# High-position tables of the S4 kernel in two tiles, one per half of a column quarter

## The chip, the cores and the metric

The kernel runs on one core of one Trainium2 chip. Its time is the device time of one execution in microseconds (us): the median of three runs is 391.03 us, the lowest 388.97 and the highest 391.36. The engines are named as in the profile: PE is TensorE, DVE is VectorE, ACT is ScalarE, POOL is GpSimd and SP is the engine that issues most of the DMAs. "SPq" and "POOLq" are the DMA queues filled from SP and POOL.

## The reference: linear attention beside an S4 convolution

The output is two independent results side by side, each 2048 x 448. The first is a hedgehog linear attention with 16 heads of 28. The second is an S4 layer: a long convolution whose kernel is a sum of 256 damped rotations for each of 448 channels.

```python
def _A_ref(x, wqkv, w_phi, wo):
    q, k, v = ...                       # x @ wqkv, split into 16 heads of 28
    pq = jnp.einsum("bhsd,hdf->bhsf", q, w_phi)
    pk = jnp.einsum("bhsd,hdf->bhsf", k, w_phi)
    phi_q = jnp.concatenate([_softmax(pq, axis=-1), _softmax(-pq, axis=-1)], axis=-1)
    phi_k = jnp.concatenate([_softmax(pk, axis=-1), _softmax(-pk, axis=-1)], axis=-1)
    kv = jnp.einsum("bhsf,bhsd->bhfd", phi_k, v)
    z  = jnp.einsum("bhsf->bhf", phi_k)
    num = jnp.einsum("bhqf,bhfd->bhqd", phi_q, kv)
    den = jnp.einsum("bhqf,bhf->bhq", phi_q, z)[..., None] + 1e-6
    return (num / den) ... @ wo

def _B_ref(u, A_re, A_im, B_re, B_im, C_re, C_im, log_dt, Dskip):
    dt = jnp.exp(log_dt)[:, None]
    logdA = dt * (A_re + 1j * A_im)
    dB = dt * (B_re + 1j * B_im)
    l = jnp.arange(L).astype(A_re.dtype)                        # bfloat16
    P = jnp.exp(logdA[:, :, None] * l[None, None, :])
    K = jnp.einsum("dn,dnl,dn->dl", Cc, P, dB).real
    y = irfft(rfft(K padded to 2L) * rfft(u padded to 2L))[:L]  # causal convolution
    return y + u * Dskip
```

The positions `l` are rounded to bfloat16 before they are used. Above 256 many of the 2048 positions therefore fall on the same value, and only 641 different positions are left. The kernel computes K at these 641 positions and lets the DFT matrices sum the repeats.

## The kernel before

**Positions.** Each of the 641 positions is the sum of a high position and a low offset, so that exp(dt A l) is a product of a high table and a low table, and the sum over the 256 states becomes a matmul: the high table is its weights, the low table is what is streamed. There are 16 high positions (16, 48, ..., 496; `HI`, L41) and 49 low offsets (`LO`, L36 to L39): plus and minus the 16 magnitudes 1 to 16 of `LO_ABS` (L33), 0, and 16 more offsets that are shifted by 512, 1024 or 1536.

**Columns.** The 448 channels are worked in four quarters (`qt`) and each quarter in two halves (`c`) of 56 channels. 128 of the 256 states lie on the partitions; the two sets of 128 are kept side by side, so a half has 112 columns and a quarter 224.

**One quarter of K** goes through these steps:

- `rotations` (L382): TensorE multiplies the angles by odd numbers (L373) and ScalarE takes sines and cosines of multiples (L389, L391) into the tile `T`, for all magnitudes. It is issued one quarter ahead.
- `dampings` (L397): TensorE again (L373), and ScalarE's exponentials go into the tile `W` (L404 for one magnitude, L407 for two or four). Two copies with a changed sign (L410, L411) follow for each half.
- `damp` (L413): VectorE multiplies exponentials by sines and cosines in place (L419), then makes the shifted offsets by multiplying with the power PW512 (L425 to L428). That completes the low tables of a half.
- `hi_tables` (L430): VectorE copies the first high position from `CB` (L433) and doubles the table four times with complex products (`cmul`, L286 to L293) by the powers PW32, PW64, PW128 and PW256. The result is `U[qt % 2][c]`: there are four tiles of 16 positions, two for the even and two for the odd quarters (L365).
- `build_k` (L444): TensorE, 224 matmuls a half (L453), with 16 columns of weights each and 49 streamed columns. Four column strips of the array hold four channels. The sums of a half lie in two PSUM tiles (`KB`, L698, set to zero once at L700), and ScalarE copies each to `Ts` (L457).
- `scatter_k` (L559): 24 DMAs bring `Ts` into the tile `Kt`, in which the positions lie on the partitions (`K_ROWS`, L42; one more row for a single position, L570).

**After K.** `kernel_spectrum` (L580) multiplies `Kt` by DFT tiles: each group of columns takes 16 tiles, seven matmuls from each (L593), and ScalarE copies the sums out (L596). The tiles are loaded by SP (`load_f`, L578) into the slots `RING` and `LATE`; four of the `LATE` slots lie directly behind the five powers in memory (L671). `conv_group` (L598) multiplies the spectra on VectorE (L610 and the sums behind it), TensorE transforms back (L634, L636), ScalarE copies out (L641) and SP stores (L645).

**The other work.** `signal_spectrum` (L217) loads blocks of u (issued by POOL), forms sums and differences on VectorE (L224, L225), and multiplies by DFT tables (L236); ScalarE or VectorE copies out (L239). Two buffers of u alternate, so a load waits for the L225 of two blocks before. `key_side` (L459) and `query_side` (L496) are the attention: in the latter, L501 and the exponentials L504 are followed by a small matmul (L510), VectorE's reciprocals (L517 on), and in each of four row blocks by matmuls (L529), VectorE's scaling (L532), a turn on TensorE (L539), a copy (L541) and the matmul with `wo` (L545).

**Order.** `rank(p)` (L679) gives the work inside it a priority. A planner goes through all instructions with these priorities and its own estimates of durations, and fixes the order of each engine before the program runs. On the chip every engine takes its instructions in that order. The ranks are: the key side 9000, the first fold of weights 8000, the high tables of quarter 0 10000, the four query sides 10500, quarter `qt` of K 11000 + 5000 `qt`, the first two kernel spectra 70000, the tail from 80000.

```python
for qt in range(4):
    with rank(11000 + 5000 * qt):
        ...
        dampings(qt)
        for c in range(2):
            damp(qt, c)
        for c in range(2):
            build_k(qt, c, Ts)
        if qt < 3:
            rotations(qt + 1)
            for c in range(2):
                hi_tables(qt + 1, c)
```

## Time and profile before

| measure | value |
|---|---|
| median of three runs | 391.03 us |
| the profiled execution: time | 391.03 us |
| the profiled execution: span, first to last instruction | 389.2 us |
| mean granted clock of TensorE | 0.855 of full speed |
| POOL busy | 34.1 us (9%) |
| matmuls of `build_k`, L453 | 1,792, 49.3 us busy |
| largest groups of VectorE: L419; L425; L610 | 37.4; 35.6; 24.4 us |
| complex products of powers and tables, L286 and L287 | 20.1 and 19.8 us |
| data moved | 31.60 MB, mean 81 GB/s |

All times inside the program are read from one profiled execution, and a time of the form "at 138.5" counts from the start of its span. The page of the profile gives for each engine its busy time and its share of the span, then the span in 40 slices with a digit of busy tenths for each engine (a slice is 9.73 us here). Groups of instructions are given by the line of the code, the engine and the operation; behind the bar stand the busy time of the group in us and the mean of one instruction in ns, then the idle time of the engine just before these instructions and the instruction that ended most of it. A row in order of time gives the start, the duration, and in brackets how long the engine had stood idle and for what. The chain of waits is followed back from the last instruction, at each step to whatever released it.

The granted clock is what the throttle allowed TensorE. It varies within the span; the mean over the span is in the table.

### The profile page before, as it was taken

The page shows a single profiled execution, that of the slowest core. Times are in us where ns is not written, and L with a number is a line of the kernel's source. Part 1 is how long each engine was busy: PE and PEld are TensorE (multiplying, and loading weights), DVE is VectorE, ACT ScalarE, POOL GpSimd, SP SyncE. Part 2 cuts the span into 40 slices and gives each one's busy share as a digit, 9 for nine tenths or more (in the row PEclk, how much of TensorE's full clock was granted, in tenths as well). Part 3 has the DMA queues.
Part 4 walks back from the last instruction along what each step waited for, and adds up shares of the span by engine and source line. Part 5 has one row for each costly group of instructions (what it writes and reads, how often), then busy time and mean ns, then how long its engine had stood idle before and what let it go on. Part 6 is the DMA issues. An engine that isn't in the chain of part 4 may idle for free.

```text
span 389.2 us, 9018 instructions
## 1 busy us (share of the span) xinstructions
PE 282.2 (73%) x3780; PEld 204.2 (52%) x3780; DVE 310.9 (80%) x548; ACT 219.1 (56%) x381; POOL 34.1 (9%) x59
## 2 busy tenths in 40 slices
PE   0294478988863859996787799677970596956994
PEld 0261353455452335674554576445860485945994
DVE  0598988999961279996459988998996979999872
ACT  1289972055554764799985846942949323212431
POOL 7100220000033000000000000001000000054000
PEclk9999569999995687999659699885986888796999
DMA  7990212200012001213000100120922218397005
GB/s 184 284 254 28 63 28 72 94 24 2 0 30 64 28 25 45 70 56 96 26 24 25 25 28 26 24 79 24 278 97 56 52 52 290 104 205 180 14 3 189
DMA packets 31105, 31.60 MB, mean 81 GB/s; under 512 B 11560, under 2 KB 28680, under 8 KB 30680
## 3 DMA queue, kind: packets, MB, share of 16 engines
q1 hardware_dynamic: 24216, 22.65, 20.1%
q0 software_dynamic: 4064, 7.23, 7.2%
q10 hardware_dynamic: 2784, 1.15, 1.3%
q8 instruction: 29, 0.48, 0.5%
q14 instruction: 12, 0.10, 0.1%
HBM read 23.07 MB, written 7.34 MB: 78 GB/s over the span
## 4 chain that ended last, share of the span: by engine, by line
PE 37%; DVE 20%; ACT 17%; DMA 11%; issue 7%; SPq 4%; POOL 3%; DVEq 0%; POOLq 0%; ACTq 0%
PE kb L453 10%; PE mmt L593 6%; DMA sbuf<-in_B_u_dram 5%; PE mmt L545 4%; PE mmt L236 3%; PE yo L634 3%; SPq L567 3%; ACT sbuf L504 3%; DVE sbuf L475 3%; DMA sbuf<-SUd 3%; PE mmt L501 3%; PE arg L373 2%; PE mmt L539 2%; DMA sbuf<-const 2%; DVE sbuf L239 2%
## 5 line engine op out<-in xcount | busy, mean ns | idle before, releaser
L453 PE MATMUL kb<-sbuf 128*16 128x49 bf16 x1792 | 49.3, 274 | 3.7 <-issue 2.9
L593 PE MATMUL mmt<-sbuf 128*128 128x112 bf16 (+1 forms) x336 | 34.4, 272 | 22.2 <-ACT sbuf L596 9.7
L419 DVE TENSOR_TENSOR sbuf<-sbuf 128x112 bf16<-128x112 bf16 (+1 forms) x64 | 37.4, 619 | 13.2 <-ACT sbuf L404 12.8
L453 PEld LDWEIGHTS <-sbuf 128*16 128x16 bf16 x1792 | 41.5, 118 | 9.4 <-issue 7.8
L236 PE MATMUL mmt<-sbuf 128*128 128x448 bf16 x128 | 34.0, 390 | 14.2 <-DVE sbuf L224 6.5
L593 PEld LDWEIGHTS <-sbuf 128*128 128x128 bf16 x336 | 28.6, 118 | 28.5 <-issue 11.2
L425 DVE TENSOR_TENSOR sbuf<-sbuf 128x896 bf16<-128x896 bf16 (+1 forms) x48 | 35.6, 775 | 0.2
L596 ACT CAST sbuf<-mmt 128x448 bf16<-128x448 f32 x32 | 16.2, 549 | 27.1 <-PE mmt L593 27.1
L634 PE MATMUL yo<-sbuf 128*128 128x112 bf16 (+1 forms) x384 | 28.8, 228 | 2.9 <-DMA sbuf<-const 1.8
L471 ACT ACTIVATE sbuf<-pkv 128x448 bf16<-128x448 f32 x32 | 15.8, 552 | 26.5 <-PE acc L485 19.1
L532 DVE TENSOR_TENSOR sbuf<-mmt,sbuf 128x448 bf16<-128x448 f32 x32 | 19.4, 622 | 11.0 <-PE mmt L529 10.7
L634 PEld LDWEIGHTS <-sbuf 128*128 128x128 bf16 x384 | 26.1, 98 | 3.5 <-DMA sbuf<-const 2.0
L610 DVE TENSOR_TENSOR sbuf<-sbuf 128x1792 bf16<-128x1792 bf16 (+1 forms) x18 | 24.4, 1400 | 3.5 <-ACT sbuf L596 3.3
L407 ACT ACTIVATE sbuf<-arg 128x896 bf16<-128x896 f32 (+1 forms) x32 | 25.8, 874 | 1.4 <-PE kb L453 1.4
L236 PEld LDWEIGHTS <-sbuf 128*128 128x128 bf16 x128 | 13.1, 106 | 19.9 <-issue 11.5
L641 ACT CAST sbuf<-yo 128x224 bf16<-128x224 f32 (+1 forms) x24 | 9.0, 410 | 25.2 <-PE yo L636 25.2
L373 PE MATMUL arg<-sbuf 128*128 128x224 bf16 x128 | 22.0, 320 | 1.3 <-ACT sbuf L404 0.7
L504 ACT ACTIVATE sbuf<-mmt 112x512 bf16<-112x512 f32 x32 | 17.2, 601 | 9.8 <-PE mmt L501 9.6
L545 PE MATMUL mmt<-sbuf 112*128 112x448 bf16 x64 | 19.6, 436 | 3.6 <-ACT sbuf L541 3.5
L501 PE MATMUL mmt<-sbuf 112*112 112x512 bf16 x64 | 19.4, 426 | 1.9 <-ACT sbuf L504 1.9
L286 DVE TENSOR_TENSOR sbuf<-sbuf 128x1792 bf16<-128x1792 bf16 (+3 forms) x33 | 20.1, 609 | 0.7
L287 DVE TENSOR_TENSOR sbuf<-sbuf 128x1792 bf16<-128x1792 bf16 (+3 forms) x33 | 19.8, 603 | 0.0
(117 smaller groups left out, 590.5 us busy)
## 6 DMA issues: line engine op xcount, KB each, us to landing
sbuf<-const SPq DMA_DIRECT2D x32, 224.0 KB
SUd<-sbuf SPq DMA_DIRECT2D x16, 224.0 KB
sbuf<-const SPq DMA_DIRECT2D x2, 1024.0 KB
sbuf<-in_A_x_dram SPq DMA_DIRECT2D x4, 448.0 KB
out_dram<-sbuf SPq DMA_DIRECT2D x16, 112.0 KB
sbuf<-SUd POOLq DMA_DIRECT2D x1, 1792.0 KB, 12.6
sbuf<-in_B_u_dram SPq DMA_DIRECT2D x4, 448.0 KB
sbuf<-SUd POOLq DMA_DIRECT2D x2, 896.0 KB, 9.2
```

The costliest lines, as they stand in the source:

```text
L236: mm(p[:, 0:D_MODEL].rearrange("p (q g x) -> p q g x", q=4, g=4), lhsT=G1[:, cp, jt, 128 * mt:128 * mt + 128], rhs=by_quarter(ab[:, cp ^ s ...
L373: mm(p[:, e // 2, (e % 2) * QC:(e % 2 + 1) * QC], lhsT=PID[:, 4 * grp + e, :], rhs=src[:, part, cols], start=(part == 0), stop=(part == 1))
L407: act(dst.rearrange("p c (a b) x -> p a b c x", b=2), src.rearrange("p a b (c x) -> p a b c x", c=2), ACT.Exp, scale=float(sgn * f))
L419: TT(out=W[:, c, cs_, r, :], in0=W[:, c, cs_ if sgn < 0 else 0, r, :], in1=T[:, cs_, j0:j0 + n, xs], op=ALU.mult)
L425: TT(out=(t2[:, :, 0:n, :], dst)[1 - i], in0=src, in1=PW[512][:, i, cols].unsqueeze(1).unsqueeze(1).to_broadcast([128, 2, n, COLS]), op=AL ...
L453: mm(p[32 * g:32 * g + N_HI, qq * N_LO:(qq + 1) * N_LO], lhsT=U[qt % 2][c][:, :, ri, xc], rhs=W[:, c, ri, :, xc], start=(i == 0), stop=(i ...
L501: mm(p[:, :], lhsT=WpQ[:, dj, 112 * c:112 * c + 112], rhs=xT[:, dj, 512 * sc:512 * sc + 512], start=(dj == 0), stop=(dj == 3))
L504: act(EQ[:, s, c, :], p[:, :], ACT.Exp, scale=1.0 - 2.0 * s)
L545: mm(pf[:, :], lhsT=oT_[:, c, :], rhs=wo[:, c, :], start=(c == 0), stop=(c == 3))
L593: mm(p[:, k2, :].rearrange("p (q g x) -> p q g x", q=nq, g=4), lhsT=f_tiles[i][1][:, fi, :], rhs=natural(Kt[:, kt, :], gi), start=(n == 0) ...
L610: TT(out=t[:, :, :], in0=su, in1=sk, op=ALU.mult)
L634: mm(p[:, k2, :], lhsT=GI[r][:, cp, mt, 128 * jt:128 * jt + 128], rhs=S[:, r, cp, mt, :], start=(cp == 0 and mt == 0), stop=False)
```

## The change

The high tables get 32 positions: the 16 of before, eight from 544 in steps of 64, and eight from 1088 in steps of 128. The last 16 are made from the first 16 by three more complex products in `hi_tables`, with the powers PW528, PW544 and PW512; the first two of these powers are new and are made once, from PW512 with PW16 and PW32. The new powers lie in memory where four `LATE` slots of the DFT tiles come later.

`U` is no longer four tiles of 16 positions, chosen by the quarter's parity and half, but two tiles of 32, one for each half. Each is rewritten for the next quarter when the matmuls of its own half have ended. The memory is the same 28,672 bytes on a partition.

The low offsets are 0 and plus and minus 24 magnitudes: the old 16 and 20, 24, 28, 32, 40, 48, 56, 64. All come from exponentials and sines of ScalarE, so `EVALS` has more rows (the fifth number is the step between target rows) and `T` holds 24 magnitudes. `damp` has no shifts by PW512 any more, and its products take 24, 15 and 9 magnitudes at a time. There are still 49 offsets.

`build_k` uses 32 columns of weights in place of 16, all 32 rows of a strip are written, and its PSUM tile is allocated anew for each half of a half; the two tiles set to zero are gone. `Kt` is filled by 28 DMAs in place of 24, since one of its row blocks comes from two runs of offsets. The DFT tiles are renumbered; each still takes seven matmuls.

```diff
-N_HI = 16
+N_HI = 32
...
-LO_ABS = [1, 3, 5, 7, 9, 11, 13, 15, 2, 6, 10, 14, 4, 12, 8, 16]
+LO_ABS = [1, 3, 5, 7, 9, 11, 13, 15, 2, 6, 10, 14, 4, 12, 8, 16, 24, 32, 40, 48, 56, 64, 20, 28]
...
-HI = [16 + 32 * a for a in range(N_HI)]
-K_ROWS = [(0, 0, 8, 0, 16), (1, 0, 8, 16, 32), (2, 8, 16, 16, 32), (3, 0, 16, 33, 41), (4, 0, 16, 41, 49)]
+HI = ([16 + 32 * a for a in range(16)] + [544 + 64 * a for a in range(8)] + [1088 + 128 * a for a in range(8)])
+K_ROWS = [(0, 0, 8, [(0, 16)]), (1, 0, 8, [(16, 32)]), (2, 8, 16, [(16, 32)]), (3, 16, 24, [(24, 36), (45, 49)]),
+          (4, 24, 32, [(28, 44)])]
...
-    PW = {k: sb(f"PW{k}", [128, 2, NCOL], BF16, oPW + 3584 * i) for i, k in enumerate((32, 64, 128, 256, 512))}
+    PW = {k: sb(f"PW{k}", [128, 2, NCOL], BF16, oPW + 3584 * i) for i, k in enumerate((32, 64, 128, 256, 512, 528, 544))}
...
     cmul(CB[:, :, :], CR[:, :, :], pw_all(16), tp[:, :, :])
+    cmul(PW[528][:, :, :], PW[512][:, :, :], pw_all(16), tp[:, :, :])
+    cmul(PW[544][:, :, :], PW[512][:, :, :], pw_all(32), tp[:, :, :])
...
-    U = [[sb(f"U{b}{c}", [128, N_HI, 2, COLS], BF16, oU + 14336 * b + 7168 * c) for c in range(2)] for b in range(2)]
+    U = [sb(f"U{c}", [128, N_HI, 2, COLS], BF16, oU + 14336 * c) for c in range(2)]
...
-    EVALS = [[(0, 4, 1, 0), (0, 4, 2, 8), (0, 2, 4, 12), (0, 1, 8, 14), (0, 1, 16, 15)], [(0, 4, 1, 4)]]
+    EVALS = [[(0, 4, 1, 0, 1), (0, 4, 2, 8, 1), (0, 2, 4, 12, 1), (2, 2, 4, 22, 1), (0, 4, 8, 14, 2), (0, 2, 16, 15, 4),
+              (0, 1, 32, 17, 1), (0, 1, 64, 21, 1)],
+             [(0, 4, 1, 4, 1)]]
...
     def dampings(qt):
...
         for c in range(2):
-            act(W[:, c, 1, 1:30:2, :], W[:, c, 0, 1:30:2, :], ACT.Copy, scale=-1.0)
-            act(W[:, c, 1, 32, :], W[:, c, 0, 32, :], ACT.Copy, scale=-1.0)
-
-    def damp(qt, c):
+            act(W[:, c, 1, 1:2 * N_ABS:2, :], W[:, c, 0, 1:2 * N_ABS:2, :], ACT.Copy, scale=-1.0)
+
+    def damp(c):
         xs = slice(c * COLS, (c + 1) * COLS)
-        n1 = N_ABS - 1
-        for j0, n, sgn in ((0, n1, -1), (n1, 1, -1), (0, n1, 1), (n1, 1, 1)):
-            r = w_rows(j0, n, sgn)
+        for j0, n, sgn in ((0, N_ABS, -1), (0, 15, 1), (15, N_ABS - 15, 1)):
+            r = w_rows(j0, n, 1, sgn)
             for cs_ in (1, 0):
                 TT(out=W[:, c, cs_, r, :], in0=W[:, c, cs_ if sgn < 0 else 0, r, :], in1=T[:, cs_, j0:j0 + n, xs], op=ALU.mult)
-        cols = slice((2 * qt + c) * COLS, (2 * qt + c + 1) * COLS)
-        for d0, s0, n in ((33, 24, 8), (41, 37, 4), (45, 41, 4)):
-            src, dst = W[:, c, :, s0:s0 + n, :], W[:, c, :, d0:d0 + n, :]
-            t2 = sb("t2", [128, 2, 8, COLS], BF16, oT2)
-            for i in (1, 0):
-                TT(out=(t2[:, :, 0:n, :], dst)[1 - i], in0=src, in1=PW[512][:, i, cols].unsqueeze(1).unsqueeze(1).to_broadcast(
-                    [128, 2, n, COLS]), op=ALU.mult)
-            TT(out=dst[:, 0], in0=dst[:, 0], in1=t2[:, 1, 0:n, :], op=ALU.add)
-            TT(out=dst[:, 1], in0=dst[:, 1], in1=t2[:, 0, 0:n, :], op=ALU.subtract)
...
     def hi_tables(qt, c):
         cols = slice((2 * qt + c) * COLS, (2 * qt + c + 1) * COLS)
-        U_ = U[qt % 2][c]
+        U_ = U[c]
...
         step(256, U_[:, 0:8], U_[:, 8:16], 8)
+        step(528, U_[:, 0:16:2], U_[:, 16:24], 8)
+        step(544, U_[:, 16:24:2], U_[:, 24:28], 4)
+        step(512, U_[:, 24:28], U_[:, 28:32], 4)
 
     def build_k(qt, c, Ts):
         for hq in range(2):
-            p = KB[hq]
+            p = ps_t.tile([128, 512], F32, name="kb", tag="kb", bufs=2)
...
-                        mm(p[32 * g:32 * g + N_HI, qq * N_LO:(qq + 1) * N_LO],
-                           lhsT=U[qt % 2][c][:, :, ri, xc],
+                        mm(p[32 * g:32 * g + 32, qq * N_LO:(qq + 1) * N_LO], lhsT=U[c][:, :, ri, xc],
                            rhs=W[:, c, ri, :, xc], start=(i == 0), stop=(i == 3), tile_position=(0, 32 * g))
...
     def scatter_k(gi, Ts, engs):
...
-        for kt, h0, h1, l0, l1 in K_ROWS:
-            for g in range(4):
-                engs[i % len(engs)].dma_start(out=dst(0, 128, kt, g), in_=Ts[32 * g + h0:32 * g + h1, l0:l1, :])
-                i += 1
+        for kt, h0, h1, runs in K_ROWS:
+            r = 0
+            for l0, l1 in runs:
+                n = (h1 - h0) * (l1 - l0)
+                for g in range(4):
+                    engs[i % len(engs)].dma_start(out=dst(r, n, kt, g), in_=Ts[32 * g + h0:32 * g + h1, l0:l1, :])
+                    i += 1
+                r += n
...
-                terms = [(0, 0), (1, 1), (2, 2), (3, 3), (4, 5)] if b == 0 else [(5, 3), (6, 4)]
+                terms = [(i, i) for i in range(5)] if b == 0 else [(5, 4), (6, 5)]
...
-    KB = [ps_t.tile([128, 512], F32, name="kb", tag="kb", bufs=2) for _ in range(2)]
-    for p in KB:
-        nc.vector.memset(p[:, :], 0.0)
```

## The prediction, made before the result was known

> **What bounds the kernel now.** I read the page's busy totals and slices first, then the groups by form, then VectorE's and ScalarE's instructions in order of time, and last the chain of waits.
>
> ```profile
> PE 282.2 (73%) x3780; PEld 204.2 (52%) x3780; DVE 310.9 (80%) x548; ACT 219.1 (56%) x381; POOL 34.1 (9%) x59
> DVE  0598988999961279996459988998996979999872
> ACT  1289972055554764799985846942949323212431
> PE 37%; DVE 20%; ACT 17%; DMA 11%; issue 7%; SPq 4%; POOL 3%; DVEq 0%; POOLq 0%; ACTq 0%
> ```
>
> No engine alone is the bound, but VectorE is full in most slices; its holes are at slices 12 to 14 (115 to 139 us) and 19 (185 to 195 us). So work added on VectorE costs its length unless it falls into a hole, and VectorE takes its instructions in order: one that waits holds all behind it.
>
> ```profile
> L419 DVE TENSOR_TENSOR sbuf<-sbuf 128x1680 bf16<-128x1680 bf16 x32 | 32.0, 1025 | 0.4 <-ACT sbuf L407 0.3
> L425 DVE TENSOR_TENSOR sbuf<-sbuf 128x896 bf16<-128x896 bf16 x32 | 18.6, 619 | 0.2
> L425 DVE TENSOR_TENSOR sbuf<-sbuf 128x1792 bf16<-128x1792 bf16 x16 | 17.0, 1086 | 0.1
> L419 DVE TENSOR_TENSOR sbuf<-sbuf 128x112 bf16<-128x112 bf16 x32 | 6.0, 212 | 12.8 <-ACT sbuf L404 12.8
> ```
>
> These are the prices: by the two L419 forms a product costs 0.154 us plus 0.5185 ns an element. The 12.8 us are the wait for ScalarE's exponentials ahead of the table products.
>
> ```profile
> 51.73 0.38 DVE L225 TENSOR_TENSOR sbuf<-sbuf 128x448 bf16<-128x448 bf16 x1
> 58.86 0.39 DVE L224 TENSOR_TENSOR sbuf<-sbuf 128x448 bf16<-128x448 bf16 x1 [0.72 <-DMA sbuf<-in_B_u_dram]
> 128.40 0.38 DVE L225 TENSOR_TENSOR sbuf<-sbuf 128x448 bf16<-128x448 bf16 x1
> 138.53 0.96 DVE L517 RECIPROCAL sbuf<-mmt 128x128 f32<-128x128 f32 x1 [2.18 <-PE mmt L510]
> 278.53 0.38 DVE L428 TENSOR_TENSOR sbuf<-sbuf 128x448 bf16<-128x448 bf16 x1
> 295.43 0.22 DVE L419 TENSOR_TENSOR sbuf<-sbuf 128x112 bf16<-128x112 bf16 x1 [3.38 <-ACT sbuf L404]
> 311.79 2.02 DVE L610 TENSOR_TENSOR sbuf<-sbuf 128x3584 bf16<-128x3584 bf16 x1
> ```
>
> These are my milestones in VectorE's time line: the load of u that waits for L225; T0, the first reciprocal of the query side, at 138.5; the end of quarter 2's low tables at 279; and the first convolution product at 311.8, which runs between the last quarter's low-table products.
>
> **The parts.** The order of instructions on each engine comes from building both kernels. Successive VectorE instructions overlap by some 0.08 us, so I count steps, not durations.
>
> *Low tables (damp).* A half drops four 1,680-element and four 112-element products and the twelve instructions of L425 to L428 (7.4 us in durations, 6.7 us in steps). It gets products of 24, 15 and 9 rows, two each (1.55, 1.03 and 0.68 us): 6.0 us in steps where there were 11.
>
> *High tables.* Three steps are added, with the shapes of the twelve dropped instructions: +6.7 us on the 7.2 us between two successive L433 copies, 14.2 us a half. So a quarter's VectorE work goes from 37 to 40.5 us. It is also moved: the old tables alternate by quarter and are written while matmuls run; the new ones wait for their own half's matmuls, with the query side's L532, and so TensorE's L539, queued behind.
>
> *PW528 and PW544.* Eight products, 6.3 us in steps, stand in VectorE's order ahead of the L225 of 51.7. That L225 releases the u load, and what follows waits on it 6.8 us later: the page shows no cover, only the 0.72 us wait. L224 comes at 66.2, not 58.9: +7.3.
>
> *Quarter 0's high tables.* 14 us are added before T0. 2 us land inside the key side, where VectorE is full (60 to 114 us). The rest fills the waits for the second block's u, but each step also stands ahead of an L225 that releases a load: last L225 +3.3 more. Two of the four L501 blocks, now early, give back 1.6. T0 is 138.5+7.3+2.0+3.3-1.6 = **149.5**.
>
> *ScalarE.* 24 magnitudes, not 16: a rotation set goes from 7.3 to 10.9 us, exponentials with sign copies from 10.1 to 15.0 (steps; the 2,688-element copy at 2.4 us is scaled from L410's 1.69). This counts only in quarter 1, where ScalarE is full from 159.6 to 201: its new stretch is 10.9+15.0, ten table loads 12.9, and 14.2 of copies and query exponentials, 53.
>
> *TensorE.* Matmuls and streamed columns stay; the weights go from 16 to 32 columns, which no row shows.
>
> ```profile
> 171.50:174.90 3.40, 3.40 (x140) 1.00 0.02 5
> 218.90:220.80 1.90, 1.90 (x78) 0.50 0.00 0
> ```
>
> These stretches hold only L453: busy us and count, then the granted clock. 24.3 ns each at clock 1.00 and at 0.50: neither streaming nor loading sets the spacing, since both would slow with the clock. A 32-column load at full clock lasts as long as a 16-column one at half. I take 0; the upper bound is the spacing once more, 5.4 us a half.
>
> The Trainium skill speaks against the change here (TensorE: Matmul & The Clock Gate, section LDWEIGHTS): a load lasts its columns over 1.2 in ns, 13.3 for 16 and 26.7 for 32; its page on TensorEngine Tiling (Restrictions) adds that column tiling excludes the fast load. Loads standing in line would by that add 13.3 ns to each of 1,792, 24 us in sum; the two stretches disagree, so my sum has none of it.
>
> *DMA.* Each scatter gets four issues more: at 13.03 us for 20 on SP, 2.6 us a scatter, 1.3 where POOL shares it; the last is covered by 28 us of convolution products ahead of its reader. Four DFT-tile loads (SP, L578, at 14.25 us) lose their free memory to PW528 and PW544. They wait for the last high tables, on SP ahead of other tile loads, but pass some 10 us before the low tables end; without that cover about 3 us. The dropped memset (1.0 us) is in a hole.
>
> **The sum**, as offsets from T0.
> 1. Quarter 0's low tables end at 19 (28.6 before). The high tables of quarter 1 wait for the halves at 25 and 37.7, but ScalarE is later: its stretch starts at 16.1 and the first sign copy ends at 69. Then 7.7 of products: quarter 1 ends at 77, 226.5 us (229.4 before).
> 2. Query side 2 comes late: reciprocal at 81.5, 3.2 of work, the half's matmuls at 86. Then high and low tables 40.5, query products 9.8, stalls behind L532 3.9: quarter 2 ends at 140, 289.5 us (279 before).
> 3. The half's matmuls: 2.2. 40.5 of tables, 1.3 for ScalarE: quarter 3 ends at 184, 333.5 us.
> 4. Its last 224 matmuls: 339.3. In the new order 53 matmuls of the first kernel spectrum (L593) come behind them, and the second convolution product needs them: 6.7 with the eviction.
> 5. The convolution then has no table work beside it: 55.6 of steps, 0.5 lost, and from the last VectorE instruction to the end 7.7, as now (381.5 to 389.2).
>
> 339.3+6.7+55.6+0.5+7.7 = 409.8 us of span. The profiled execution took 391.03 at a span of 389.2 and is the median, so 1.8 is added: **411 us**, 5% slower.
>
> **Rivals.**
> *A: the shorter path pays (faster).* From the exponentials to the matmuls there are now 12 us of products a quarter, 22 before; the rewriting could fall wholly into ScalarE's 15 us of exponentials. Of the 184 us of offset 3, VectorE works 158. With no idle time there the end is 26 us earlier, 385 us; it decides below 1.5 us of idle. For it: the hole of slice 19. Against it: the high tables begin only when matmuls end that wait for the low tables. 0.05. With up to 9 us of idle it ends between 387 and 395: 0.07.
> *B: part of the stalls vanish*, or the u loads arrive sooner than their 6.8 us: 395 to 403, 0.12.
> *C: the 32-column load sets the spacing.* Each half's matmuls would last up to 5.4 longer where VectorE waits (offsets 86 and 142, and both last halves): 16 us, 427. The trace speaks against it at clock 1.00, not below. 0.10.
> *D: the wait isn't by halves.* If the first high table waited for both halves, the rewriting would start some 5.5 later in quarters 2 and 3: 422. The order shows one wait on TensorE at each L433, which can't tell the two apart. 0.04.
> *Forecast*, 403 to 419: 0.62.
>
> A difference of 1% is about what this measurement can tell. Faster is A, 0.05; the same 0.07; slower B, C, D and the forecast, 0.88. The range of 8 in 10 is 396 to 424: the forecast, nearly all of B, and C and D as far as 424. All bounds add up outside it: the weights at their upper bound reach 427, idle at nothing 385.
>
> **What would show it.** L224 of the first block near 66 and the first L517 near 150; L453 at 24 ns a matmul; each L433 of quarters 2 and 3 idle on L453 by 1 to 3 us; L610's second instruction waiting some 10 us for L596; VectorE full from there to the last store. I am wrong if the first L517 is below 145, if L433 waits for nothing, or if convolution products again run between table products.

## The result and the profile after

The changed kernel takes **414.74 us** (median of four runs, 413.13 to 415.87) where the kernel before takes 391.19 beside it (388.97 to 392.51). The ratio is 1.0605, with an interval of 1.0539 to 1.0671: 6% slower. All ratios here leave out executions that are over 1.5% above the fastest of their kernel, so they can differ a little from the ratio of the medians. The profiled execution took 415.81 us at a span of 414.0.

Line numbers moved with the edit: L224 and L225 are now L228 and L229, L389 and L391 (the sines) are L397 and L399, L404 and L407 are L416 and L419, L410 and L411 are one L423, L419 is L430, L433 is L435, L453 and L457 are L458 and L461, L517 is L521, L532 is L536, L593 and L596 are L601 and L604, L610 is L618.

First the page of the changed kernel: busy totals, two rows of slices, and the shares of the chain that ended last.

```profile
PE 287.3 (69%) x3780; PEld 206.8 (50%) x3780; DVE 330.1 (80%) x538; ACT 252.2 (61%) x433; POOL 35.5 (9%) x61
...
DVE  0599995999996568399959589989559995996992
ACT  1399962145537694899997889932769723205331
...
PE 34%; ACT 24%; DVE 20%; DMA 11%; issue 7%; POOL 2%; SPq 1%; DVEq 0%; ACTq 0%; POOLq 0%
```

VectorE has 19.2 us more work and its share of the span is still 80%: it also idles 5.6 us more. ScalarE has 33.1 us more, and on the chain its part went from 17% to 24% (66 to 99 us) while VectorE's stayed at 20%. In the slices (10.35 us each, counted from 0) ScalarE is nearly full from 16 to 25, 166 to 269 us: `8999978899`. That is a first hint against a forecast that followed VectorE nearly everywhere, and no more than that: the chain is only one path.

The groups by form, busy time and mean ns of one, then idle time ahead of them:

```profile
L430 DVE TENSOR_TENSOR sbuf<-sbuf 128x2688 bf16<-128x2688 bf16 x16 | 24.4, 1555 | 0.0
L430 DVE TENSOR_TENSOR sbuf<-sbuf 128x1680 bf16<-128x1680 bf16 x16 | 16.4, 1026 | 0.0
L430 DVE TENSOR_TENSOR sbuf<-sbuf 128x1008 bf16<-128x1008 bf16 x16 | 10.6, 677 | 0.7 <-ACT sbuf L416 0.7
L435 DVE COPY sbuf<-sbuf 128x224 bf16<-128x224 bf16 x8 | 1.7, 218 | 10.3 <-PE kb L458 10.3
```

The three products cost 1.56, 1.03 and 0.68 us, as worked out. The wait for ScalarE ahead of them went from 12.8 to 0.7 us, and a wait of 10.3 us for TensorE stands in its place, ahead of the copy that begins each high table (0.7 us before).

VectorE's time line, each row with its start, its length and, in brackets, the idle time ahead of it:

```profile
58.81 0.39 DVE L229 TENSOR_TENSOR sbuf<-sbuf 128x448 bf16<-128x448 bf16 x1
66.18 0.39 DVE L228 TENSOR_TENSOR sbuf<-sbuf 128x448 bf16<-128x448 bf16 x1 [2.22 <-DMA sbuf<-in_B_u_dram]
...
148.07 0.96 DVE L521 RECIPROCAL sbuf<-mmt 128x128 f32<-128x128 f32 x1 [5.47 <-PE mmt L514]
...
292.87 0.22 DVE L435 COPY sbuf<-sbuf 128x224 bf16<-128x224 bf16 x1 [3.38 <-PE kb L458]
...
304.31 0.22 DVE L435 COPY sbuf<-sbuf 128x224 bf16<-128x224 bf16 x1 [5.06 <-PE kb L458]
...
332.90 6.11 DVE L430 TENSOR_TENSOR sbuf<-sbuf 128x2688 bf16<-128x2688 bf16 x6
339.76 3.96 DVE L618 TENSOR_TENSOR sbuf<-sbuf 128x3584 bf16<-128x3584 bf16 x2 [0.76 <-ACT sbuf L604]
346.07 2.02 DVE L633 TENSOR_TENSOR sbuf<-sbuf 128x3584 bf16<-128x3584 bf16 x1 [2.35 <-DMA sbuf<-in_B_u_dram]
...
352.97 3.96 DVE L618 TENSOR_TENSOR sbuf<-sbuf 128x3584 bf16<-128x3584 bf16 x2 [2.60 <-ACT sbuf L604]
```

These are the milestones again. The u load of the first block lands 7.3 us later, T0 is at 148.1, quarter 3's two high tables wait 3.4 and 5.1 us, and the convolution's products come behind all of quarter 3's tables. From this line, by stages (the last VectorE instruction ends at 405.9):

| stage | before, us | forecast | after | change forecast | change measured |
|---|---|---|---|---|---|
| start to T0 | 138.5 | 149.5 | 148.1 | +11.0 | +9.6 |
| T0 to the end of quarter 2's low tables | 140.4 | 140.0 | 141.4 | -0.4 | +1.0 |
| from there to the end of quarter 3's | 51.1 | 44.0 | 49.5 | -7.1 | -1.6 |
| from there to the last VectorE instruction | 51.5 | 68.6 | 66.9 | +17.1 | +15.4 |
| to the end of the span | 7.7 | 7.7 | 8.1 | 0 | +0.4 |
| sum | 389.2 | 409.8 | 414.0 | +20.6 | +24.8 |

The stage that was sized wrong is quarter 3's: 9.6 us of idle time on VectorE where I had 3.5. The same stage on TensorE and then on ScalarE:

```profile
287.75 6.82 PE L458 MATMUL kb<-sbuf 128*32 128x49 bf16 x273
297.02 3.33 PE L458 MATMUL kb<-sbuf 128*32 128x49 bf16 x128 [2.46 <-issue]
303.49 0.77 PE L458 MATMUL kb<-sbuf 128*32 128x49 bf16 x23 [3.15 <-issue]
...
327.17 4.15 PE L601 MATMUL mmt<-sbuf 128*128 128x224 bf16 x28 [15.13 <-ACT sbuf L604]
```

```profile
290.63 1.28 ACT L397 ACT_TABLE_LOAD   x1
...
310.36 1.28 ACT L419 ACT_TABLE_LOAD   x1
...
321.68 5.01 ACT L423 ACTIVATE sbuf<-sbuf 128x2688 bf16<-128x2688 bf16 x2
326.35 1.21 ACT L604 CAST sbuf<-mmt 128x448 bf16<-128x448 f32 x2
```

TensorE stops twice inside quarter 2's matmuls, 2.46 and 3.15 us, with no semaphore to wait for ("issue"; the last section says what ends such a stop). Then the first kernel spectrum, L601, stands still for 15.1 us: its sums must be copied out by ScalarE's L604, and that lies behind a block that runs from 290.6 to 326.7 us, sines, exponentials and sign copies of quarter 3. In this block ScalarE also waits 5.9 us for the sums of quarter 2's matmuls (2.3 and 3.6 us, ahead of two copies L461), so TensorE's stops are part of its length. In the kernel before, ScalarE's time line has the last part of that block, exponentials and sign copies, shorter (13.2 us from the table load on, against 16.3) and earlier:

```profile
287.12 1.28 ACT L407 ACT_TABLE_LOAD   x1
...
299.92 0.41 ACT L411 ACTIVATE sbuf<-sbuf 128x112 bf16<-128x112 bf16 x1
300.11 1.08 ACT L596 CAST sbuf<-mmt 128x448 bf16<-128x448 f32 x2
```

So two theories could account for the loss. **V**, that of the prediction: VectorE's order sets the time, by the added products in front, the added steps and the waits of L435. **S**: ScalarE's longer block sets it, by the ends of the quarters and by the spectrum's copies. A third, **Q**, adds the stops of TensorE beside the bulk loads. The experiments take these apart.

### The profile page after: what moved, and what is told of

Its sections match the earlier page's. It is cut to its first block, busy times and chain, and to the rows that moved or that the text cites. A ratio compares the mean times of both kernels' runs of the same rounds, so it can differ in the third digit from the quotient of the medians.

```text
span 414.0 us, 9072 instructions
## 1 busy us (share of the span) xinstructions
PE 287.3 (69%) x3780; PEld 206.8 (50%) x3780; DVE 330.1 (80%) x538; ACT 252.2 (61%) x433; POOL 35.5 (9%) x61
## 3 DMA queue, kind: packets, MB, share of 16 engines
q1 hardware_dynamic: 24136, 22.65, 18.6%
## 4 chain that ended last, share of the span: by engine, by line
PE 34%; ACT 24%; DVE 20%; DMA 11%; issue 7%; POOL 2%; SPq 1%; DVEq 0%; ACTq 0%; POOLq 0%
PE kb L458 11%; DMA sbuf<-in_B_u_dram 6%; PE mmt L240 5%; ACT sbuf L419 4%; PE mmt L549 3%; PE mmt L601 2%; DVE sbuf L430 2%; DVE sbuf L618 2%; PE mmt L543 2%; PE mmt L505 2%; DMA sbuf<-const 2%; DVE sbuf L291 2%; ACT sbuf L508 2%; DVE sbuf L290 2%; DMA sbuf<-sbuf 2%
## 5 line engine op out<-in xcount | busy, mean ns | idle before, releaser
L458 PE MATMUL kb<-sbuf 128*32 128x49 bf16 x1792 | 52.3, 279 | 6.3 <-issue 6.1
L458 PEld LDWEIGHTS <-sbuf 128*32 128x32 bf16 x1792 | 44.3, 142 | 13.7 <-issue 12.1
L430 DVE TENSOR_TENSOR sbuf<-sbuf 128x1008 bf16<-128x1008 bf16 (+2 forms) x48 | 50.0, 1086 | 0.8 <-ACT sbuf L416 0.7
L601 PE MATMUL mmt<-sbuf 128*128 128x112 bf16 (+1 forms) x336 | 30.6, 252 | 27.2 <-ACT sbuf L604 16.8
L240 PE MATMUL mmt<-sbuf 128*128 128x448 bf16 x128 | 36.4, 414 | 13.2 <-DVE sbuf L228 5.1
L290 DVE TENSOR_TENSOR sbuf<-sbuf 128x896 bf16<-128x896 bf16 (+3 forms) x59 | 40.9, 693 | 1.1
L601 PEld LDWEIGHTS <-sbuf 128*128 128x128 bf16 x336 | 25.6, 108 | 32.2 <-issue 19.6
L291 DVE TENSOR_TENSOR sbuf<-sbuf 128x896 bf16<-128x896 bf16 (+3 forms) x59 | 40.3, 687 | 0.0
L419 ACT ACTIVATE sbuf<-arg 128x896 bf16<-128x896 f32 (+1 forms) x52 | 37.6, 813 | 0.0
L536 DVE TENSOR_TENSOR sbuf<-mmt,sbuf 128x448 bf16<-128x448 f32 x32 | 19.5, 623 | 16.3 <-PE mmt L533 16.1
L604 ACT CAST sbuf<-mmt 128x448 bf16<-128x448 f32 x32 | 15.8, 551 | 25.6 <-PE mmt L601 25.5
L642 PE MATMUL yo<-sbuf 128*128 128x112 bf16 (+1 forms) x384 | 30.1, 231 | 1.7 <-DVE sbuf L629 1.7
L397 ACT ACTIVATE sbuf<-arg,sbuf 128x896 bf16<-128x896 f32 (+2 forms) x36 | 27.8, 778 | 0.1
L642 PEld LDWEIGHTS <-sbuf 128*128 128x128 bf16 x384 | 26.6, 99 | 2.0 <-DVE sbuf L629 1.8
L618 DVE TENSOR_TENSOR sbuf<-sbuf 128x1792 bf16<-128x1792 bf16 (+1 forms) x18 | 24.3, 1401 | 3.4 <-ACT sbuf L604 3.4
L296 DVE TENSOR_TENSOR sbuf<-sbuf 128x448 bf16<-128x448 bf16 (+3 forms) x59 | 25.0, 423 | 1.1
L240 PEld LDWEIGHTS <-sbuf 128*128 128x128 bf16 x128 | 13.7, 111 | 23.9 <-issue 16.7
L399 ACT ACTIVATE sbuf<-arg 128x896 bf16<-128x896 f32 (+2 forms) x36 | 24.8, 695 | 0.1
L297 DVE TENSOR_TENSOR sbuf<-sbuf 128x448 bf16<-128x448 bf16 (+3 forms) x59 | 24.7, 419 | 0.0
```

The lines of the kernel that those rows point to most:

```text
L240: mm(p[:, 0:D_MODEL].rearrange("p (q g x) -> p q g x", q=4, g=4), lhsT=G1[:, cp, jt, 128 * mt:128 * mt + 128], rhs=by_quarter(ab[:, cp ^ s ...
L290: TT(out=tmp, in0=src, in1=pw(1), op=ALU.mult)
L291: TT(out=dst, in0=src, in1=pw(0), op=ALU.mult)
L397: act(dst, src, ACT.Sin, scale=float(f), bias=bias_hp[:, :])
L419: act(dst.rearrange("p c (a b) x -> p a b c x", b=2), src.rearrange("p a b (c x) -> p a b c x", c=2), ACT.Exp, scale=float(sgn * f))
L430: TT(out=W[:, c, cs_, r, :], in0=W[:, c, cs_ if sgn < 0 else 0, r, :], in1=T[:, cs_, j0:j0 + n, xs], op=ALU.mult)
```

## The experiments

Twelve kernels ran. Where the kernel before was run with them its median was 388.97 to 390.3 us. "P" stands for the eight products that make PW528 and PW544.

### The products in front, alone, in the kernel before

```diff
 cmul(CB[:, :, :], CR[:, :, :], pw_all(16), tp[:, :, :])
+cmul(PW[528][:, :, :], PW[512][:, :, :], pw_all(16), tp[:, :, :])
+cmul(PW[544][:, :, :], PW[512][:, :, :], pw_all(32), tp[:, :, :])
```

> The kernel before, with only the eight products for PW528 and PW544 added in the place that the changed kernel gives them; nothing reads them. My theory: they push back the L225 that releases a load of u, nothing hides them, and the first reciprocal of the query side (138.5 us before) comes 5 to 7.5 us later; the time is 396 to 399 us. The rival, that VectorE's hole at 115 to 139 us takes the delay up: the reciprocal stays within 1.5 us of 138.5, and the time within 2 us of 391.

Measured: 397.91 us (396.01 to 399.81), ratio 1.0206 (1.0125 to 1.0286). VectorE's time line of this kernel:

```profile
58.85 0.38 DVE L225 TENSOR_TENSOR sbuf<-sbuf 128x448 bf16<-128x448 bf16 x1
...
66.54 0.39 DVE L224 TENSOR_TENSOR sbuf<-sbuf 128x448 bf16<-128x448 bf16 x1 [2.55 <-DMA sbuf<-in_B_u_dram]
...
147.11 0.96 DVE L519 RECIPROCAL sbuf<-mmt 128x128 f32<-128x128 f32 x1 [2.18 <-PE mmt L512]
```

The step held. L225 comes at 58.9, not 51.7, the L224 behind its load at 66.5, not 58.9, T0 at 147.1, not 138.5, and the medians differ by 8.5 us, so all of it reaches the end (by the interval 5 to 11 us).

### The products late, in the changed kernel

```diff
-cmul(PW[528] ...); cmul(PW[544] ...)      # behind CB's
+with rank(9500):                          # behind the key side's rank
+    cmul(PW[528] ...); cmul(PW[544] ...)
```

> The changed kernel, with the eight products moved behind the first block's sums of u (rank 9500, just ahead of quarter 0's high tables). My theory: the last L228 of the first block goes from 66.2 back to 59 us, the key side is full on VectorE and takes some 2 to 4 us of the products back, so the first reciprocal comes 3 to 6 us earlier than 148.1 and the time is 409 to 412 us. The rival, that the front's delay is made by the high tables' extra steps and not by the place of the products: the reciprocal stays within 1.5 us, and the time at 413 to 416.

Measured: 413.50 us (412.18 to 413.80), ratio 1.0594 (1.0510 to 1.0678). T0 does move, from 148.1 to 140.7. Of these 7.4 us, 2.0 are left at the last VectorE instruction (403.9 against 405.9), and the medians differ by 1.2, which is less than their intervals. My time missed. The rival's (413 to 416) held, though its case for the reciprocal didn't. This is the first crack in V: the same products cost 8.5 us in the kernel before and next to nothing in the changed one, so there something else is late behind them.

### Two tiles alone, in the kernel before

```diff
-U = [[sb(f"U{b}{c}", ..., oU + 14336 * b + 7168 * c) for c in range(2)] for b in range(2)]
+U = [sb(f"U{c}", ..., oU + 14336 * c) for c in range(2)]
-U_ = U[qt % 2][c]
+U_ = U[c]
```

> The kernel before with its 16 high positions, but with two tiles in place of four: each half's tile is rewritten when its own half's matmuls end. This is the wait of the change without its extra work. My theory: VectorE's copies L433 of quarters 1 to 3 wait for L453 by 1 to 4 us each where before they waited 0.7 us in sum; a part of it falls into the 12.8 us that VectorE waits for exponentials anyway; the time is 393 to 399 us. One rival: the rewriting fits wholly into the waits for ScalarE, and the time stays within 2 us of 391. The other: the wait is most of the 24 us, and the time is over 403.

Measured: 390.09 us (387.25 to 391.29, ten runs), ratio 1.0012 (0.9978 to 1.0047). The waits of this kernel, in all, times, longest:

```profile
DVE sbuf L433 <- PE kb L453: 12.6, 4, 5.1
...
DVE sbuf L419 <- ACT sbuf L404: 9.5, 2, 7.2
```

Alone, in the kernel before, the edit that gives the change its name costs nothing that can be measured. Its wait is there in full, 12.6 us on the matmuls where 0.7 stood, and the time stays. Later waits shrink by half of it: for ScalarE's exponentials from 12.8 to 9.5 us, for L529's matmuls from 10.7 to 8.2. Quarter 2 ends 4.6 us later, quarter 3 only 1.5, and the last VectorE instruction is not late at all. The rival's case, that the rewriting fits wholly, held, and my number missed. Four tiles in the changed kernel were not tried.

### The bulk loads at the end of quarter 2, moved

TensorE's stops lie beside two loads of 1,792 and 1,024 KB that POOL issues at 288.4 and 290.8 us. Two kernels move them. In the first both stand at the end of the program's text, on SP:

```diff
-                load_su(0)
-                nc.gpsimd.dma_start(out=GI[0][:, :, :, :], in_=GI_d[0])
+    load_su(0, nc.sync)
+    nc.sync.dma_start(out=GI[0][:, :, :, :], in_=GI_d[0])
```

> The changed kernel, with the first 1.8 MB load of the spectrum of u and the 1 MB load of the first inverse table issued by SP behind the scatter of the second quarter in place of by POOL at 288 and 291 us. In the changed kernel the matmuls L458 of quarter 2 stand still for 2.5 and 3.2 us with no releaser but 'issue' while these loads fill the DMA engines, and the copies L435 of quarter 3 wait 3.4 and 5.1 us for them. My theory: TensorE's instructions come late because the loads hold the DMA engines; without them there, the two L435 wait 1 to 3 us together, and the time falls by 3 to 6 us to 409 to 412, less what the loads cost where they land now. The rival, that TensorE waits for ScalarE's copy of the sums: the stalls stay, and the time is 413 to 417.

Measured: 411.72 us (410.33 to 415.81), ratio 1.0577 (1.0489 to 1.0665). The planner moved the second load alone (321.9); the first went out at 286.4. One stop stays, 2.64 us, the other is gone, and the second wait of L435 is 2.27, not 5.06. The median falls by 3 us, about what that wait lost, but the intervals of the two ratios overlap, so a gain isn't shown.

In the second kernel both loads wait for quarter 2's last matmuls, by two copies of one element that ScalarE makes after them:

```diff
+            if qt == 2:
+                for first in (SU[0][:, 0, 0, 0, 0, 0:1], GI[0][:, 0, 0, 0:1]):
+                    nc.scalar.copy(first, Ts[:, 0, 27:28])
```

> The changed kernel, with the two loads (1.8 MB of the spectrum of u, 1 MB of the inverse table) held back by two one-element copies of ScalarE that stand behind the last eviction of quarter 2: so they start after all L458 of quarter 2. (Moving them to SP's queue had moved the second load alone, and one of the two stalls went with it.) My theory, that the stalls of L458 are TensorE's instructions arriving late while the loads hold the DMA engines: both stalls go, the second L435 of quarter 3 waits under 1 us where it waited 5.1, the first still 3.4, and the time is 408 to 411 us. The rival, that the stalls wait for an eviction or belong to the matmuls themselves: both stay and the time is 413 to 416.

Measured: 421.11 us (418.59 to 422.56), ratio 1.0795 (1.0737 to 1.0853). TensorE's time line of this kernel:

```profile
273.19 5.64 PE L458 MATMUL kb<-sbuf 128*32 128x49 bf16 x224 [8.65 <-DVE sbuf L430]
279.20 5.86 PE L458 MATMUL kb<-sbuf 128*32 128x49 bf16 x224 [0.37 <-DVE sbuf L430]
...
340.43 1.10 PE L458 MATMUL kb<-sbuf 128*32 128x49 bf16 x34 [3.42 <-issue]
...
359.28 6.85 PE L601 MATMUL mmt<-sbuf 128*128 128x224 bf16 x70 [11.27 <-DMA sbuf<-const]
```

Both stops are gone, each half's 224 matmuls run through, quarter 3's low tables end at 325.7, 13.3 us earlier, and the kernel is 6 us slower. A stop of 3.42 us shows up in quarter 3, where other bulk transfers now run, and VectorE waits 26.9 us for the spectrum's copies (L618 on L604). The last and longest of these waits, 15.0 us, has a cause of its own: the copy waits for L601's matmuls, they wait 11.3 us for a DFT tile, and SP issues that tile's load at 356.6, behind quarter 3's scatter, which fills SP from 342.1 to 356.4. In the changed kernel the tiles of the first spectrum come ahead of that scatter. So this run shows that the loads beside the stops are not the whole loss, and it can't show whether an earlier end of quarter 3 would pay: what it gained is lost again behind the scatter. How much of the time Q explains stays open.

### ScalarE's added work taken away, in the changed kernel

The magnitudes above 16 are evaluated in quarter 0 only. The sines, exponentials and sign copies of the other quarters are those of the kernel before; VectorE, TensorE and the tables' shapes stay, and the upper rows are not evaluated anew, so the kernel computes other values:

```diff
+    OLD_EVALS = [[(0, 4, 1, 0, 1), (0, 4, 2, 8, 1), (0, 2, 4, 12, 1), (0, 1, 8, 14, 1), (0, 1, 16, 15, 1)], [(0, 4, 1, 4, 1)]]
-            for e0, n, f, r0, st in EVALS[grp]:
+            for e0, n, f, r0, st in (OLD_EVALS if qt else EVALS)[grp]:      # twice
+            m = 2 * N_ABS if qt == 0 else 32                                # sign copies
```

> The changed kernel, with ScalarE's sines, exponentials and sign copies of the eight new magnitudes done for quarter 0 only; quarters 1 to 3 use what is left there from before, so this computes other values. It takes 8.5 us of ScalarE out of each of these quarters and nothing from VectorE. My theory: ScalarE sets the end of quarter 1's low tables (228 us in the changed kernel) and not of quarters 2 and 3, where VectorE does; quarter 1 ends 6 to 9 us earlier and most of that lasts to the end, 406 to 410 us. The rival, that VectorE sets quarter 1 too: 413 to 416. Another, that ScalarE sets all three: under 400.

Measured: **393.63 us** (392.63 to 394.98), ratio 1.0113 (1.0071 to 1.0155): 4 us above the kernel before, where the changed kernel stands 24 above it. From its page, the busy totals and the chain's shares:

```profile
PE 283.2 (72%) x3780; PEld 204.7 (52%) x3780; DVE 327.1 (84%) x538; ACT 219.4 (56%) x382; POOL 35.4 (9%) x61
...
DVE 40%; PE 34%; ACT 11%; issue 6%; DMA 5%; POOL 2%; DVEq 0%; ACTq 0%; POOLq 0%
```

VectorE still has 327 us of work. The windows show where the time went; each row has the busy time of PE, its loads, DVE, ACT and POOL in one stretch, then the granted clock, the DMA share and GB/s. First the kernel before, then the changed one, then this one, each from the end of quarter 2's low tables to the last VectorE instruction:

```profile
278.90:381.50 102.60, 74.60 (x1408) 67.30 (x1400) 92.27 (x133) 40.63 (x83) 10.19 (x14) 0.85 0.41 115
```

```profile
289.50:405.90 116.40, 79.48 (x1526) 71.97 (x1518) 97.04 (x132) 56.02 (x105) 12.68 (x18) 0.81 0.45 125
```

```profile
143.70:283.80 140.10, 114.80 (x1720) 77.61 (x1717) 115.77 (x203) 90.71 (x143) 0.72 (x2) 0.83 0.13 39
...
283.80:381.10 97.30, 71.19 (x1383) 65.75 (x1381) 96.85 (x135) 45.35 (x88) 13.53 (x18) 0.93 0.52 151
```

With 97 us of VectorE work in both, the changed kernel takes 116.4 us for this stretch and this one 97.3: its VectorE has 0.45 us of idle time where the changed kernel's has 19.4. In the stretch ahead, T0 to the end of quarter 2, nothing was gained: 140.1 us against 141.4. S holds as far as the time goes, and the gain isn't in quarter 1, where I had counted ScalarE, but behind quarter 2.

What is gone there can be read from VectorE's waits. Of the 19.4 us of idle time in the changed kernel, 8.4 are L435's two waits for quarter 2's matmuls, 3.7 wait for the inverse transform's sums (L630 on L642), 3.4 for the spectrum's copies (L618 on L604) and 2.6 for loads of u (L633). So only a small part of it names ScalarE. The largest part goes back to quarter 2, where the first product of the low tables runs 20 us earlier with the light exponentials, 4.4 of them from T0 (first row the changed kernel, second row this one):

```profile
268.00 1.03 DVE L430 TENSOR_TENSOR sbuf<-sbuf 128x1680 bf16<-128x1680 bf16 x1
```

```profile
247.59 0.68 DVE L433 TENSOR_TENSOR sbuf<-sbuf 128x1008 bf16<-128x1008 bf16 x1
```

ScalarE's sign copies for quarter 2 end at 270.5 in the changed kernel and at 259.2 here. Here half of quarter 2's 448 matmuls run between 268.2 and 281, and quarter 3's copies into the high tables (L438 here) wait for nothing. In the changed kernel nearly all of them run behind 287.7. The order of the instructions differs too, so this is a reading of two traces and not a proof.

### VectorE's added steps taken away, in the changed kernel

The three steps of the high tables run in quarter 0 only; the upper 16 positions keep quarter 0's values:

```diff
+        if qt == 0:
             step(528, ...); step(544, ...); step(512, ...)
```

> The changed kernel, with the three added steps of the high tables (528, 544, 512) done in quarter 0 only; quarters 1 to 3 read the rows left from it, so this computes other values. It takes 13.4 us of VectorE out of each of quarters 1 to 3. My theory: nothing in quarter 1, where ScalarE is later; in quarters 2 and 3 the end of the low tables comes up to 13 us and some 10 us earlier, until ScalarE is the limit there too; 391 to 402 us. A rival, that the wait for the half's matmuls sets these quarters and not the work behind it: over 408. Another, that VectorE sets all three quarters: under 386.

Measured: 408.55 us (404.29 to 410.55), ratio 1.0457 (1.0378 to 1.0536). The page of this kernel (its profiled execution, at 410.55, was the longest of the four, so its times are on the long side):

```profile
PE 285.6 (70%) x3780; PEld 206.8 (51%) x3780; DVE 291.1 (71%) x466; ACT 252.6 (62%) x433; POOL 35.4 (9%) x61
```

39 us of VectorE's work are gone and 6 us of the time. Quarter 3's low tables end at 320.4, 18.6 earlier, but the first convolution products that need the second half of the spectrum start at 349.9, against 353.0. (I call these the second convolution product.) VectorE waits 13.5 us there for the spectrum's copies, and here too a DFT tile stands behind them:

```profile
342.60 7.11 PE L602 MATMUL mmt<-sbuf 128*128 128x224 bf16 x42 [6.69 <-DMA sbuf<-const]
```

SP issues that load at 339.9, behind quarter 3's scatter, which starts at 328.1. So a part of what the missing steps gained is taken back by SP's order, and the 6 us are not the full price of the steps. The opposite cut, in quarter 0:

```diff
+        if qt > 0:
             step(528, ...); step(544, ...); step(512, ...)
+        else:
+            nc.vector.tensor_copy(U_[:, 16:32], U_[:, 0:16])      # in place of the steps: other values
```

> The changed kernel, with one plain copy of the lower 16 positions in place of the three added steps in quarter 0 alone, so this computes other values: some 13.4 us less of VectorE ahead of the query side, and one or two us of copies more. My theory: the steps cost 3 to 5 us in the first reciprocal of the query side (148.1 us), part in the full key side and part ahead of the sums that release loads of u; the time is 409 to 412 us. The rival, that the hole at 115 to 139 us takes them: reciprocal and time within 1.5 us of the changed kernel's.

Measured: 415.89 us (413.75 to 416.62), ratio 1.0673 (1.0626 to 1.0721). T0 is 144.5, 3.6 earlier, and the end isn't. Quarter 0's steps cost nothing at the end that can be measured.

### ScalarE's added work, alone, in the kernel before

Two extra sines of four magnitudes for each of sine and cosine, two extra exponentials of four for each sign, and a 448-element copy a half, each quarter, into memory that nobody reads (the first `LATE` slot, before its DFT tile is loaded):

```diff
+    MORE = [(0, 4, 8), (0, 4, 4)]
+    spare = sb("spare", [128, 4 * QC], BF16, oPW + 17920)
+            if grp == 0:                       # rotations; the same with Exp in dampings
+                for e0, n, f in MORE:
+                    for cs_ in range(2):
+                        act(dst, src, ACT.Sin, scale=float(f), bias=bias_hp[:, :])
+            act(spare[:, 0:2 * QC], W[:, c, 0, 0:4, :].rearrange("p a x -> p (a x)"), ACT.Copy, scale=-1.0)
```

> The kernel before, with ScalarE's added work alone: two more four-magnitude sines twice a set, two more four-magnitude exponentials twice and two more copies a quarter, written to spare memory that nothing reads; some 3.8 us a set of sines and 4.9 us a quarter of the rest, against the 3.6 and 4.9 us that the change adds. My theory now, after the changed kernel without this work in quarters 1 to 3 took 393.6 us: ScalarE's added work is the largest single part of the loss; 400 to 410 us. The rival, that it is hidden beside VectorE here, and that taking it out of the changed kernel helped by another order of the instructions: within 3 us of 390.

Measured: **413.14 us** (409.95 to 415.48), ratio 1.0636 (1.0549 to 1.0722). From its page the busy totals and the chain's shares, and from its waits three of VectorE's (lines moved: L435 is L419, L533 is L517, L548 is L532):

```profile
PE 284.2 (70%) x3780; PEld 206.8 (51%) x3780; DVE 311.7 (76%) x548; ACT 257.8 (63%) x427; POOL 34.1 (8%) x59
...
DVE 28%; PE 26%; ACT 24%; DMA 11%; issue 7%; POOL 3%; DVEq 0%; SPq 0%; ACTq 0%; POOLq 0%
```

```profile
DVE sbuf L548 <- PE mmt L545: 22.5, 17, 3.8
...
DVE sbuf L533 <- PE mmt L526: 12.8, 4, 9.2
...
DVE sbuf L435 <- ACT sbuf L413: 9.8, 4, 6.1
```

With not one VectorE instruction added, ScalarE's work alone costs as much as the whole change, 24 us, and more than was expected of it. Its place is another one: T0 to the end of quarter 2 takes 170.1 us against 140.4, and the stretch behind takes 94.4 against 102.6. A part of that is order: a convolution product of 2.0 us, with a wait of 3.3 us for the spectrum's copies ahead of it, here stands in front of quarter 2's last table products. VectorE waits 12 us more for L529's matmuls (L548 here) and 6.5 more for the query side's sums (L533), both fed by ScalarE's copies and exponentials. ScalarE is 5.6 us busier here than in the changed kernel, so the price is slightly too high as a copy of it.

### Can ScalarE be relieved?

Three kernels try. The sign copies go to VectorE, in the changed kernel and in the kernel before; and in the kernel before, besides, quarter 1's rotations get one rank, so that the planner sets them in a block and ScalarE loads its tables 9 times, not 17:

```diff
-            act(W[:, c, 1, 1:2 * N_ABS:2, :], W[:, c, 0, 1:2 * N_ABS:2, :], ACT.Copy, scale=-1.0)
+            nc.vector.tensor_scalar_mul(W[:, c, 1, 1:2 * N_ABS:2, :], W[:, c, 0, 1:2 * N_ABS:2, :], -1.0)
```

> The changed kernel, with the sign copies done by VectorE in place of ScalarE. ScalarE loses eight copies of 2.59 us (20 us in all), VectorE gains eight of some 0.8 us (a copy of 3,584 elements took it 1.09 us). My theory, that ScalarE's exponentials and copies are what the end of each quarter's low tables waits for: 5.2 us a quarter go from the path and 1.7 come back on VectorE; 402 to 408 us. The rival, that VectorE's work sets the quarters: its 6.6 us are added and nothing is gained, 414 to 421.

> The same in the kernel before: ScalarE loses 16.4 us (eight copies of 1.69 and eight of 0.37 us), VectorE gains some 5 us. VectorE waited 12.8 us for the exponentials there, not for the copies. If ScalarE's block is on the path, 384 to 389 us and faster than both kernels; if VectorE's own work sets the time, 391 to 396.

```diff
-                rotations(qt + 1)
+                with rank(10400 if qt == 0 else tc.cur_priority):
+                    rotations(qt + 1)
```

> The kernel before, with the sign copies on VectorE as in the run above (387.6 us) and with the sines of quarter 1 given the rank 10400: ScalarE's order then has them in one block ahead of the second query side's exponentials, in place of alternating with them, and eight of seventeen table loads of 1.28 us go. If ScalarE's stretch in quarter 1 is on the path, as the two runs with more and with less of its work say, a good part of those 10.3 us is gained: 378 to 385 us, faster than both kernels. The rival, that quarter 1 has slack on ScalarE in the kernel before and only the added work uses it up: 386 to 389.

Measured: 415.55 us (415.37 to 417.00), ratio 1.0686 (1.0621 to 1.0750) for the changed kernel; 387.62 (385.63 to 391.78, ten runs), ratio 0.9968 (0.9929 to 1.0007), and 390.44 (387.09 to 391.98), ratio 1.0016 (0.9970 to 1.0062) for the two of the kernel before. The first was a miss: ScalarE is 17.8 us less busy (234.4 against 252.2), and none of the time is gone. The copies in the changed kernel were not the part of the block that matters, or VectorE, which now makes them at 0.86 us each, took over the delay; these runs can't say which. In the kernel before, 23 us less work than ScalarE's 219 moves nothing that can be measured, where 39 us more cost 24. No kernel here beats the one before beyond its interval.

## Why the prediction was right, and where it was not

The time (411 against 414.7) and the sign were right. The stages of the sum came out within 1.4 us up to the end of quarter 2, and the path that the sum follows is there in the trace. What the sum didn't see is how much of the loss ScalarE's added work makes.

- **The products in front: right.** L228 at 66.18 against 66.2, and alone they cost 8.5 us, against 7.3 in the sum. That they keep this price in the changed kernel was wrong: there they are worth 1 to 2 us.
- **T0: right as a number, 148.1 against 149.5.** Its small terms aren't shown one by one. Three kernels whose engines take the same instructions in the same order up to there (the changed one and the two with the loads moved) have T0 at 148.1, 146.9 and 143.3, so terms of 2 to 5 us lie within what one execution differs from the next. The match within 1.4 us is partly luck.
- **VectorE's prices: right** (1.56, 1.03, 0.68 us a product; quarter 0 to 2 stages within 1.4 us of the forecast).
- **ScalarE's sizes: right.** The exponentials with sign copies take 14.7 us from 311.65 to 326.35, against 15.0 in the sum; the last sign copy of quarter 1's first half ends 70.9 us behind T0, against 69.
- **"The convolution follows quarter 3's end": right.** VectorE waits 0.5 us between the second L435 at 304.3 and the end of quarter 3's low tables at 339.0. The last 224 matmuls end at 346.4, and 53 matmuls of the first spectrum follow, as forecast. The second convolution product starts at 353.0, 14.0 us behind the tables, where the sum has 12.5. It waits 2.6 us for the copy and not some 10, since two other products and two products of u fill the time before.
- **"This counts only in quarter 1": the step that failed.** In quarter 1, where I counted ScalarE, its lighter work gained nothing: T0 to the end of quarter 1 is 82.6 us in that kernel and 79.8 in the changed one. What it gained is behind quarter 2: 19.1 of the 24.8 us between the two profiled executions' last VectorE instructions, with 4.4 at T0, which may be chance. I had let ScalarE go from quarter 2 on. There its longer exponentials put the first low-table product at 268.0 (247.6 with the light ones), and by the reading above L435's waits follow from that; and I had never followed it as the engine that copies out the first kernel spectrum, which the convolution needs. The second convolution product starts at 349 to 355 us in the variants with the full sines and exponentials (362 with both loads held back), and at 325.7 with the light ones. That it stays late even where quarter 3 ends 18.6 and 13.3 us earlier isn't shown to be ScalarE's doing: in those two kernels it waits for a DFT tile behind the scatter.
- **The wait of L435: right in kind, too small in quarter 3.** About 1.2 us in quarter 2 (forecast 3.9 with all stalls there), 8.4 in quarter 3 against 2.2. The second of the two waits there, 5.1 us, is no longer than TensorE's two stops ahead of it, 5.6. This is the mis-sized term of the sum; its 6.2 us are more than the 4.2 between the forecast's span and the measured one, and the other stages take the rest back. Alone, in the kernel before, the wait costs nothing at 12.6 us, so its length says little about its price.
- **"The convolution has no table work beside it": right** (339.8 is behind the last table product). That VectorE would be full from there on was wrong: it is busy 57.1 of 66.9 us.

Of the rivals, **A** (the path gets shorter) is half right, in that the rewriting alone, in the kernel before, does fit beside other work, but nothing was freed by it. **B** (stalls vanish, or u comes sooner) didn't come: L228's wait for u is 2.2 us where it was 0.7, and L435's waits grew. **C** (the 32-column load sets the spacing) is refuted. These stretches of the changed kernel, and of the one with the late products, hold L458 alone (busy us and count, then the granted clock):

```profile
184.50:187.20 2.70, 2.70 (x110) 1.00 0.03 6
332.60:336.50 3.90, 3.90 (x163) 1.00 0.41 128
```

```profile
284.60:286.00 1.40, 1.40 (x61) 0.50 0.00 0
```

24.5 and 23.9 ns at full clock and 23.0 at half, as with 16 columns (24.3). The loads' own records did get longer, from 118 to 142 ns on the mean (first row the kernel before, second row the changed one):

```profile
L453 PEld LDWEIGHTS <-sbuf 128*16 128x16 bf16 x1792 | 41.5, 118 | 9.4 <-issue 7.8
```

```profile
L458 PEld LDWEIGHTS <-sbuf 128*32 128x32 bf16 x1792 | 44.3, 142 | 13.7 <-issue 12.1
```

These loads overlap each other, and the matmuls don't come further apart. So the prediction's 0 ns was right, but its argument wasn't: in its two stretches of the kernel before, a load's record has 118 ns at clock 1.00 and 118 at 0.50, so the loads did not slow with the clock, and an equal spacing says nothing of them. An estimate from the Trainium skill (TensorE: Matmul & The Clock Gate, section LDWEIGHTS) makes each load 13.3 ns longer. The trace's records grew by 24, and no trace here shows either in the spacing, so the measurement decides. **D** (the wait isn't by halves) is refuted as well: quarter 3's first L435 starts at 292.87, when some 224 of quarter 2's 448 matmuls are through, and its second half's run until 304.3.

**What stays open.** Taking work away or adding it lets the planner write another order. In the kernel with light ScalarE, half of quarter 2's matmuls are spread over the time before 281 us, no stop shows, and the spectrum comes elsewhere; with ScalarE heavy in the kernel before the loss falls into quarters 1 and 2. So it is shown that the time comes and goes with ScalarE's added work, by most of the 24 us, and not how much of that is its duration and how much the order that the planner makes of it. The prices don't add up either: alone in the kernel before, products 8.5, two tiles 0.6 and ScalarE 24.2 are 33 us without VectorE's steps, and the whole change costs 24. A kernel with the same order and shorter ScalarE instructions wasn't tried, nor one without the steps in which the DFT tiles stay ahead of the scatter.

## What to carry to other kernels

When an edit makes an engine's block longer, follow not only who waits for the block's own results but every instruction queued behind it on that engine, above all the small copies that set PSUM free: here a block of tables held up the first kernel spectrum by 15 us, though by itself that doesn't show what it cost. A wait that shows up after a change isn't yet a price: 12.6 us of it cost nothing where other waits shrank, and the same eight products cost 8.5 us in one kernel and 1 to 2 in another. A cheap test is to add the suspected engine's load alone to the old kernel, and to take it away alone from the new one; if both move the time by about the whole difference, that load is where to look first. Then look whether the order of the instructions moved as well, on the queue of the DMAs too: in two kernels here a tile's load fell behind a scatter and took back a part of what the edit had gained.

## What was not expected of the hardware

- **TensorE stops in the middle of its own independent matmuls, and what it waits for is instructions.** The view calls these stops "issue", since no semaphore ends them. The traces' DMA packets show what does: twelve of the fourteen traces have 19 such stops of over 0.9 us, up to 3.44, and each ends 1.27 to 1.61 us after the landing of a 16,384-byte packet that the trace marks as instructions (queue q8, 29 of them in each trace). In the changed kernel these packets land at 295.59 and 302.16 us, and the matmuls go on at 297.02 and 303.49; between the two stops lie 128 matmuls with their 128 loads. Other packets of this kind land without a stop. The stops at 294.6 and 300.3 come while the core's DMA engines move about 300 GB/s, or have just done so; when both loads were held back both stops went, and one came up just after other transfers (3.42 us before 340.4, behind 4 us at 333 GB/s). That the bulk transfers are what makes these packets late isn't shown.
- **The spacing of these column-tiled matmuls didn't care for the width of the weights**, 16 or 32 columns, nor for the granted clock, 0.50 or 1.00: 23 to 24.5 ns, while the loads' records went from 118 to 142 ns.
- **VectorE makes the sign copy of 2,688 bf16 elements in 0.86 us, ScalarE in 2.59** (means of eight), and eight fewer of ScalarE's table loads, at 1.28 us each, gained nothing.
